# Another order table for a three-layer attention and MLP kernel on one core

## The chip, the cores and the metric

The kernel runs on one core of one Trainium2 chip. The time is the device time of one execution in microseconds. The kernel before takes 849.13 us (median of 3 runs, 848.77 to 849.22).

Six things work side by side in a core. TensorE (PE) multiplies matrices; its weight loads are listed as PEld. VectorE (DVE), ScalarE (ACT) and GpSimd (POOL) work element by element. SyncE (SP) issues the transfers of this kernel, and 16 DMA engines carry them out. Each engine works through its own list of instructions in order; an instruction that needs another engine's result waits at the head of its list, and everything behind it waits too.

## The reference, cut to what matters

```python
# q, k, v: (4, 8, 576, 64) float32
scores = (1/8) * q @ k.T
# heads 0-3: the last 32 positions; heads 4-7: every 4th of the last 128
scores = where(mask, scores, -1e9)
attn = softmax(scores)                        # over keys, + 1e-9 in the denominator
x = attn @ v                                  # -> (2304, 512)
h = x @ w_in;  g = relu(h)**2;      y1  = g @ w_out     # 512 -> 2048 -> 512
h = y1 @ w_in2; g = h*sigmoid(h);   out = g @ w_out2    # 512 -> 2048 -> 512
```

The four weight matrices come as 64-bit floats.

## The kernel before, in words

**Attention.** The 4 x 576 positions are eight halves of 288; each half has four pairs of heads, so there are 32 blocks. Of a block the kernel loads q, k and v (`load_blk`), multiplies q and k on TensorE (L533, "scores"), adds the mask and takes the row's extreme on VectorE (L558), exponentiates on ScalarE (L566, or L729 after a transpose for the first eight blocks), scales (L573, L575, L586, L590, L592, L754), transposes on TensorE (L602, L713, L715, L717) and multiplies by v (L625, L738). The first blocks subtract the extreme before the transpose (`less`, L691 on VectorE, L694 on GpSimd). Attention's matmuls are in fp32.

**Weights.** A piece of 128 x 512 weights arrives as 64-bit numbers (`raw`) and is turned into two fp32r parts, a high and a low one, whose sum it is (`weights`): the exponent and mantissa words are converted (L282 and L290 on ScalarE, L284 and L292 on VectorE or GpSimd), shifted (L302, or L304 on GpSimd), given their sign (L311, L314), added (L318), copied as the high part (L245 on ScalarE, L247 on VectorE, L249 on GpSimd: the helper `copy`) and subtracted for the low part (L252: the helper `sub`).

**First MLP.** Tiles of 256 tokens, three of them side by side (`mlp`): 12 fp32r matmuls of 256 columns per step S1 (L788 to L790: high x high, high x low, low x high), relu and square, split into high and low (L245, L252), and 12 per step S2 (L836 to L838). Attention and the conversion of weights run beside it. Then three tiles of 512 tokens (`mlp2`, L936, L990 to L992), in which products of sums of blocks save matmuls; the second MLP's weights are prepared at that time.

**Second MLP.** Three tiles of 768 tokens (`strassen`), with seven block products for eight, in steps of six matmuls of 384 columns (L1094 first, L1179 second product). Its halves are copied (L245, ScalarE) and subtracted (L252, VectorE or GpSimd; tiles `hl` and `gq`); prepared weights stream in as `ws`, `wa`, `wc` and `sw`.

**Order.** All this is 3,960 numbered operations. Nothing is planned when the kernel is built: a table, `ORDER`, lists them. `V1318` says that operation 1318 is issued to VectorE at this place of the program; A is ScalarE, G GpSimd, P TensorE, D a transfer on SP's queue. Numbers behind `@` are places of the buffers that the operation opens: a PSUM bank, or a place in a ring of SBUF. `F14@0` is a group of 14 warm-up matmuls on zeros (`filler`, L1245). A GpSimd operation also waits for the last VectorE operation before it in the table that is marked with `lock`. Waits between engines, and for a buffer's old readers, are derived from the tiles. So the table alone sets each engine's list, and which engine an operation goes to where several can do it.

Of the kernel before, what the change touches and what calls it, by code (L numbers as in the profile page):

```python
# [1358 lines left out]
V1 A3958 G0 F14@0 D3@140 D2@132 D33@136 V4 D64@144 D126@24 P5@20@0 F15@2 V8 V7 D34@148 V6 V18 D135@32 V9 V19  # L1359
P10@3 P36@28@1 V17 V50 P67@36@2 G20 A12 V38 A11 V49 V37 D65@156 V48 P13@0 V39 V68 V40 D95@152 P21@1 F3@3 V51 A22  # L1360
P41@2 A23 D96@160 V35 V14 P24@3 V71 A43 V15 G127@0 V70 A42 A16@2 V81 D398@196 V79 P52@1 V69 V82 P44@2 V80 A53
V25 A54 V72 A136@4 P55@0 V26 V45 V66 V46 A27 V83 D143@52 P98@40@3 V56 V138 A47@6 V57 P28@1 G129 P73@3 V100
A29@44 F3@2 V58 A74 V101 D160@76 P59@2 V111 A31@48 V99 P84@3 V32 A62 V30 A60 P75@0 A85 V102 V61 A128 F3@1 V63
V110 D152@56 P86@2 V76 V103 A137 V77 V112 P104@1 A78@8 V113 V87 F7@3 V97 V114 V88 A105 V130 D177@88 A89 P115@1
V139 P106@0 A116 V131 F1@2 P90@3 D169@80 P117@2 V140 A91@60 A93@64 A132@68 F5@1 V94 V92 A141@164 V107 V118
P400@3@1@72@0 V108 V119 D211@124 G133 A153@14 V109@12 V120 A162 V403 F2@2 V401 A145 P121@0 G142 V402 V410
D506@201 P404@2 V411 A122 A144@10 V123 V412 A154 V146 P1238@3 D186@92 V399 A161@2 V147 A170@0 V148 P413@1 A124
A405 V178@4 D220@128 A149@84 V125 V163 A1239@16 P406@0 V150 A414 A1240 V164 P415@2 A179 D194@108 V407 V155
P1244@3 A1241@6 V408 V165 A409@8 V416 V156 A166@100 D424@196 P507@0@1@96@1 V417 V1242 A418 V157 P1243 A1245@18
V167 A158@168 D151 V172 A1246 V510 A187@10 D134 P419@3 V159 P1250@2 A422@104 A420 V512 A1247@12 G189 V508 V423  # L1370
A513 V421 A171 D203@116 V1248 P426@3@0@112@2 V180 A1251@16 V173 A511 P1249 A509 V427 G174 V523 A1252 V428 A188
V429 V436 V438 A1253@14 P430@2 V525 A524 V437 V514 V521 A526 V515 V425 V1254 A522 P439@1 V190 A431 A516 V527
A517 V175@172 P432@3 V528 V176 A440 A529 P518@0 V530 A222 P441@2 V433 V181 A204@2 P531@1 P1255 V434 V442 A520
V182 A435@8 V443 V519 A533 V444 D539@196 A532 A183@120 V191 P534@3 A195@6 V184 P445@0 A537@12 A535 V446 P1256@1
A192@176 G197 V448 V536 A196 V447 D450@201 V449 V198 A205 V193 A1257@18 P540@0@3@20@3 A1258 V199 A1259@4 D237@40
A212@0 V1260 V554 A200@28 P1261 V556 G206 V545 A557 V558 V543 A555 D254@76 V541 V201 A559 P452@0@3@24@0 A542
V560 V207 A544 A546 V561 D538 V451 P1262@1 V208 D271@112 A562 A563 V547 V465 V548 V455 A549 V466 G550 V454
P564@2 V463 A1263@16 D228@36 V464 A565 V456 A1264 V453 A566 V209@180 P551@1 A1265@8 V214 P457@2 A552 A553 V210
A221@14 D245@72 P567@1 V215 A458 A213 V223 P467@0 V1266 A238@12 V216 P459@3 A568 A468 V224 D572@196 A570@4
A217@32 P469@2 V240 A229@10 V225 P1267 A256 V460 V470 V461 V471 G218 V462@6 A239 D478@201 V472 A246@8 V569  # L1380
P473@0 V231 P1274@1 A476@52 A474 V241 A230 V475 A226@184 D262@92 V477 V232 P573@3@0@56@1 A1275@18 V227 A1276
A1277@2 V233 D296@116 A255@6 P480@1@2@80@2 V589 V587 A234@88 G1278 V580 V593 V576 A590 V574 G235 V591 P1279 A247
V483 D305@24 V484 V482 A592 V481 V493 A575 V492 V494 A581 P485@0 V578 V491 A577 D202 V248 A588 V263@10 P495@3
A579 V242 A486 A594 V582 P1286@0 A243@188 V583 D279@108 V479 V595 V584 A272@0 V596 V249 P585@1 V597 A1287@16
P487@2 D219 V244 A586 A496 P598@1 V250 A1288 D571 P497@3 D288@124 A599 V488 A1289@2 V489 P600@0 A490@14 V498
# [288 lines left out]
```

## Time and profile before

| | |
|---|---|
| median of 3 runs | 849.13 us |
| profiled execution | 849.5 us |
| its span, first to last instruction | 847.7 us |
| busy: PE, DVE, ACT, POOL | 839.2, 638.8, 501.5, 122.2 us |
| DMA | 223.56 MB, 264 GB/s on average |

A span is the time between the first and the last instruction. Busy time is a union: instructions of one engine overlap at their ends. An engine's idle time matters only where another waits for it.

### The profile page before, as it was taken

The numbers are of one execution on the slowest core, as the hardware profiler recorded it, in microseconds if no ns is written. First come the engines' busy times: TensorE is split into PE (matmuls) and PEld (weight loads), VectorE is DVE, ScalarE is ACT, GpSimd is POOL, SyncE is SP. The second block draws the span as 40 slices with busy tenths as digits, with TensorE's granted clock in tenths as the row PEclk, the third lists the DMA queues.
The fourth block names the chain that finished last, engine by engine and source line by source line (L and its number), as shares of the span: only waits on it lengthen the run. The fifth ranks groups of instructions, "written<-read, shape, count | busy, mean of one in ns | idle before, by whom it ended". The sixth has DMA issues, their size and how long they took to land.

```text
span 847.7 us, 16967 instructions
## 1 busy us (share of the span) xinstructions
PE 839.2 (99%) x6009; PEld 795.6 (94%) x6009; DVE 638.8 (75%) x1706; ACT 501.5 (59%) x1324; POOL 122.2 (14%) x142
## 2 busy tenths in 40 slices
PE   9989999999999999999999999999999999999998
PEld 7879999999989889889998999999999999999998
DVE  6999999888888698768899997578722488422765
ACT  5999988887666265334542566565445555345652
POOL 2220000101210202131201002102201111202020
PEclk9999999999999999999999999999999999999999
DMA  9585568879898888988999989889774774773441
GB/s 344 178 284 207 152 204 304 278 265 333 310 303 318 308 292 282 326 311 288 336 344 299 343 308 351 301 287 324 248 259 149 246 266 164 269 262 111 174 159 65
DMA packets 83603, 223.56 MB, mean 264 GB/s; under 512 B 8768, under 2 KB 18240, under 8 KB 83520
## 3 DMA queue, kind: packets, MB, share of 16 engines
q1 hardware_dynamic: 83520, 222.49, 75.2%
q8 instruction: 47, 0.77, 0.3%
q14 instruction: 36, 0.29, 0.1%
HBM read 172.13 MB, written 50.33 MB: 262 GB/s over the span
## 4 chain that ended last, share of the span: by engine, by line
PE 94%; ACT 3%; DVE 1%; issue 0%; POOL 0%; POOLq 0%; ACTq 0%
PE y L1094 17%; PE sa L1179 15%; PE s L936 15%; PE y L1179 6%; PE y L990 5%; PE y L991 5%; PE y L992 5%; PE sa L1094 4%; PE s L788 3%; PE s L789 2%; PE s L790 2%; PE ax L533 2%; PE y L836 2%; PE ax L625 2%; PE y L837 2%; PE y L838 2%
## 5 line engine op out<-in xcount | busy, mean ns | idle before, releaser
L245 ACT CAST hl<-gq 128x384 fp32r<-128x384 f32 x168 | 79.5, 513 | 58.7 <-PE sa L1179 28.6
L1094 PE MATMUL y<-xs,ws 128*128 128x384 f32 x552 | 107.5, 334 | 0.0
L252 DVE TENSOR_TENSOR hl<-gq,hl 128x384 fp32r<-128x384 f32 x144 | 78.9, 581 | 27.3 <-ACT hl L245 24.0
L1094 PEld LDWEIGHTS y<-xs,ws 128*128 128x128 f32 x552 | 96.6, 188 | 0.1
L1065 DVE TENSOR_TENSOR gq<-y,gq 128x384 f32<-128x384 f32 x46 | 25.0, 554 | 94.1 <-PE y L1094 82.9
L1070 ACT COPY gq<-y 128x384 f32<-128x384 f32 x92 | 42.7, 479 | 75.0 <-PE y L1094 67.6
L1179 PE MATMUL sa<-hl,wp 128*128 128x384 f32 x432 | 79.1, 334 | 0.0
L936 PE MATMUL s<-x,ws 128*128 128x256 f32 x576 | 76.2, 284 | 0.0
L990 PE MATMUL y<-g,w 128*128 128x512 f32 x192 | 76.2, 397 | 0.0
L1179 PEld LDWEIGHTS sa<-hl,wp 128*128 128x128 f32 x432 | 75.2, 188 | 0.0
L991 PE MATMUL y<-g,w 128*128 128x512 f32 x192 | 75.2, 392 | 0.0
L992 PE MATMUL y<-g,w 128*128 128x512 f32 x192 | 74.9, 390 | 0.0
L952 DVE TENSOR_TENSOR h<-s,h 128x512 f32<-128x512 f32 x96 | 59.4, 619 | 19.8 <-PE s L936 16.6
L936 PEld LDWEIGHTS s<-x,ws 128*128 128x128 f32 x576 | 72.2, 191 | 1.2
L245 ACT CAST g<-r 128x256 fp32r<-128x256 f32 (+1 forms) x86 | 42.9, 504 | 51.2 <-DVE r L972 42.8
L566 ACT ACTIVATE ap<-ap,ast 96x128 f32<-96x128 f32 (+3 forms) x168 | 62.2, 371 | 8.3 <-DVE ast L575 4.2
L788 PE MATMUL s<-x,w 128*128 128x256 f32 x192 | 56.4, 294 | 0.1
L790 PE MATMUL s<-x,w 128*128 128x256 f32 x192 | 54.3, 283 | 0.0
L789 PE MATMUL s<-x,w 128*128 128x256 f32 x192 | 54.2, 282 | 0.0
L1179 PE MATMUL y<-hl,sw 128*128 128x384 f32 x288 | 51.4, 334 | 0.0
L1179 PE MATMUL sa<-hl,sw 128*128 128x384 f32 x288 | 50.9, 334 | 0.0
L1179 PEld LDWEIGHTS y<-hl,sw 128*128 128x128 f32 x288 | 50.0, 188 | 0.0
(176 smaller groups left out, 2071.2 us busy)
## 6 DMA issues: line engine op xcount, KB each, us to landing
raw<-w SPq DMA_DIRECT2D x64, 512.0 KB, 6.3
ws<-w1x SPq DMA_DIRECT2D x48, 512.0 KB, 6.7
ws<-w2x SPq DMA_DIRECT2D x48, 512.0 KB, 5.4
sw<-w2y SPq DMA_DIRECT2D x48, 512.0 KB, 4.5
wa<-w1s SPq DMA_DIRECT2D x24, 512.0 KB, 6.8
wa<-w2s SPq DMA_DIRECT2D x24, 512.0 KB, 5.7
w1x<-st SPq DMA_DIRECT2D x16, 512.0 KB, 4.8
w2x<-st SPq DMA_DIRECT2D x16, 512.0 KB, 5.1
```

The source lines that it names most:

```text
L245: self.nc.scalar.copy(out=out, in_=in_)
L252: self.eng[eng].tensor_tensor(out=out, in0=a, in1=b, op=ALU.subtract)
L566: es.append(self.op({"ACT": c_act(nk) + 0.185}, lambda e, i=i, n=n, c=c, p=p, st=st: nc.scalar.activation(out=p.tile[:n, c], in_=p.tile[:n ...
L788: nc.tensor.matmul(o, wh.tile[:, s], xh, start=(kk == 0), stop=False)
L789: nc.tensor.matmul(o, wh.tile[:, s], xl, start=False, stop=False)
L790: nc.tensor.matmul(o, wl.tile[:, s], xh, start=False, stop=(kk == KC - 1))
L936: nc.tensor.matmul(bank.tile[:, o:o + 256], wp, xp, start=i == 0, stop=last, skip_group_check=True)
L990: nc.tensor.matmul(o, wh.tile[:, s], gh.tile, start=c == 0, stop=False)
L991: nc.tensor.matmul(o, wh.tile[:, s], gl.tile, start=False, stop=False)
L992: nc.tensor.matmul(o, wl.tile[:, s], gh.tile, start=False, stop=(c == NF - 1))
L1094: nc.tensor.matmul(o, w[part == 2].tile[:, kk * P:kk * P + P], x[b][part == 1].tile[:, kk * half:kk * half + half], start=new and not kk a ...
L1179: nc.tensor.matmul(o, u.tile[:, c * P:c * P + P], v.tile, start=new and not q and not part, stop=q == nf - 1 and part == 2, skip_group_che ...
```

## The change

The table `ORDER` is replaced by another one; nothing else in the file differs. Each of the 3,960 operations is still there once. The 516 transfers stand in the same order as before. 180 operations are on another engine: 73 from ScalarE to VectorE, 55 from VectorE to ScalarE, 43 from GpSimd to VectorE, 9 from GpSimd to ScalarE. Of the 750 operations of TensorE 316 stand at another place in its list. The groups of warm-up matmuls have 45 matmuls in all, before 53. Most places of buffers are others. The start and the end of the table, before and after:

```diff
 ORDER = """
-V1 A3958 G0 F14@0 D3@140 D2@132 D33@136 V4 D64@144 D126@24 P5@20@0 F15@2 V8 V7 D34@148 V6 V18 D135@32 V9 V19
-P10@3 P36@28@1 V17 V50 P67@36@2 G20 A12 V38 A11 V49 V37 D65@156 V48 P13@0 V39 V68 V40 D95@152 P21@1 F3@3 V51 A22
...
+V1 F11@2 D3@111 D2@195 P5@13@0 G0 V6 V7 V8 V9 V17 V18 V19 D33@68 P36@88@1 V39 V37 D64@133 F11@1 V20 P21@1 A3958
...
-A3946@202 A3956 D3947 D3957
+V3932 P3929 P3933 P3937 D3911 D3913 D3847 P3941 P3945 P3948 P3949 A3946@83 D3947 P3950 P3951 P3952 P3953 P3954
+P3955 A3956 D3957
 """
```

In these lines 5, 36 and 67 are the scores of the first three blocks, 10 and 21 transposes of the first block, 12 and 22 exponentials, 20 the subtraction of the extreme of the first block's second head.

## Rows read from the trace of the kernel before

**Rows 1.** The page's first part: busy us, share of the span, instructions of each engine.
```profile
PE 839.2 (99%) x6009; PEld 795.6 (94%) x6009; DVE 638.8 (75%) x1706; ACT 501.5 (59%) x1324; POOL 122.2 (14%) x142
```
**Rows 2.** Stretches: length, busy PE, PEld, DVE, ACT, POOL, clock, DMA share, GB/s.
```profile
7.00:20.00 13.00, 12.41 (x155) 10.63 (x154) 10.96 (x81) 8.90 (x36) 3.33 (x5) 1.00 1.03 403
20.00:80.00 60.00, 56.64 (x579) 51.92 (x576) 58.37 (x248) 57.30 (x180) 10.52 (x12) 1.00 0.71 244
80.00:220.00 140.00, 139.88 (x1298) 134.12 (x1298) 128.41 (x414) 117.71 (x381) 6.08 (x10) 1.00 0.73 249
220.00:380.00 160.00, 160.00 (x1236) 142.28 (x1235) 126.75 (x383) 77.49 (x260) 33.38 (x41) 1.00 0.88 309
380.00:500.00 120.00, 120.00 (x734) 108.62 (x733) 110.39 (x192) 53.97 (x99) 14.12 (x18) 1.00 0.91 316
500.00:840.00 340.00, 340.00 (x1963) 339.91 (x1962) 202.42 (x382) 183.72 (x366) 53.11 (x47) 1.00 0.67 232
```
**Rows 3.** Waits of PE: line, waited for; us in total, times, longest.
```profile
PE y L837 <- POOL g L252: 0.9, 1, 0.9
PE y L836 <- ACT g L245: 0.8, 1, 0.8
```
**Rows 4.** Chain of waits in the last stage: start, us, what.
```profile
627.85 6.24 PE y L1094 x36
```
**Rows 5.** Timeline of the first 14 us, vector engines: start, us, what [idle before].
```profile
5.72 0.29 DVE L558 CUSTOM_DVE_ANT_0 ap<-y,mask 96x128 f32<-96x128 f32 x1 [2.39 <-PE y L533]
...
5.93 0.28 DVE L558 CUSTOM_DVE_ANT_0 ap<-y,mask 96x128 f32<-96x128 f32 x1
...
7.61 2.00 POOL L694 TENSOR_SCALAR ap<-ap,ast 96x96 f32<-96x96 f32 x3 [5.15 <-DVE ast L558]
...
9.11 0.29 DVE L558 CUSTOM_DVE_ANT_0 ap<-y,mask 96x128 f32<-96x128 f32 x1 [1.60 <-PE y L533]
...
10.58 0.47 ACT L729 ACTIVATE ap<-ax 96x96 f32<-96x96 f32 x2 [1.80 <-PE ax L713]
```
**Rows 6.** Timeline of the first 14 us, PE: warm-up matmuls, scores, transposes.
```profile
0.98 3.17 PE L1245 MATMUL fill<-warm 128*128 128x256 bf16 x14 [0.98 <-DVE warm L1237]
...
4.09 1.49 PE L533 MATMUL y<-w 64*96 64x96 f32 x12
5.51 2.52 PE L1245 MATMUL fill<-warm 128*128 128x256 bf16 x15
7.87 0.41 PE L713 MATMUL ax<-ident,ap 96*128 96x96 f32 x3
```
**Rows 7.** Timeline of PE where it turns between attention and MLP.
```profile
97.19 0.39 PE L788 MATMUL s<-x,w 128*128 128x256 f32 x1
97.41 0.28 PE L789 MATMUL s<-x,w 128*128 128x256 f32 x1
97.53 0.28 PE L790 MATMUL s<-x,w 128*128 128x256 f32 x1
...
245.16 0.87 PE L936 MATMUL s<-x,wc 128*128 128x256 f32 x6
245.96 0.72 PE L625 MATMUL ax<-ap,blk 96*64 96x96 f32 x12
```
**Rows 8.** Groups by line and form: busy us, mean ns of one, idle before.
```profile
L284 DVE TENSOR_SCALAR cv<-raw 128x512 f32<-128x512 f32 x18 | 7.5, 419 | 2.6 <-DMA raw<-w 2.3 <-PE zx L838 0.3
L290 ACT ACTIVATE raw<-raw 128x512 int32<-128x512 uint32 x50 | 33.2, 679 | 2.9 <-DMA raw<-w 2.9
L252 DVE TENSOR_TENSOR hl<-gq,hl 128x384 fp32r<-128x384 f32 x144 | 78.9, 581 | 27.3 <-ACT hl L245 24.0 <-POOL hl L252 2.7
L252 POOL TENSOR_TENSOR hl<-gq,hl 128x384 fp32r<-128x384 f32 x24 | 25.7, 1076 | 155.2 <-DVE hl L252 53.5 <-ACT hl L245 45.2 <-DMA wa<-w2s 33.6
```
**Rows 9.** Transfers into tile sw: us from issue to landing.
```profile
DMA to landing us min/median/max: 3.5/4.5/9.9
```

More of the change, by code (lines that the diff above doesn't have):

```diff
@@ L1364 @@
[L1364 to L1373, printed above, removed]
@@ new lines @@
+A1299@153 A1300 A297@148 V603@156 V257 V265 V258 V503 V290 V505 P1268@3 A1269@146 A1270 A1271@5 D605@73
+P606@2@1@14@3 V602 V274 V275 D638@9 A298 A264 P1280@0 A1281@93 V259 V620 V622 V624 V626 V1272 V607 A608 A260@192
+A1282 A1283@41 G1284 V282 V609 V283 V613 V261 V266 P1292@3 D322@56 D604 A1293@22 A289@108 D313@80 P639@1@36@2
+V641 V645 V611 V273 P640@0 V654 V291 A1301@201 A1294 A324 A614 A1295@146 A306@0 A610 V1551@7 V267 V643 A612 A646
+P1273 P1285 A642 A644 P1304@1 A621 V1302 V284 V1296 A268@128 A307 A655 V285@40 V652 V656 V615 V269 A623
@@ new lines @@
+A1305@150 A625 P1303 A657 A627 A653 P1310@2 V616 V617 P618@3 V286 V299 V647 V1550@162 V276 V658 V659 P1322@0
+V628 V629 P1297 D339@124 D185 A619 A1306 A1311@94 A1307@138 A1312 V648 A649 A660 V1554@156 V630 P631@2 A632
+V1308 P1309 V1552@110 V308 A277@132 V292 D666@201 V1553 V293 V278 V294@136 D287 A1323@153 P661@3 A1313@5 A1324
+A1325@151 V1326 P633@1 P650@2 V300 V1314 V295 V301 A651 A636@21 A662 A634 A315 P1316@0 A1317@116 D637
+P667@3@76@1 V671 P668@2 A1318 A1319@20 P663@0 V684 A1556 A664@93 V669 V635 V673 V682 A685 V680 V1320 V1555 P1315
@@ new lines @@
+A865 P1459 D2079 D2080@76 D909@196 P1430@2 A1431@90 V1639 V1641 V1632 P877@3 A878 P879@3 V1650 V1651 A1432
+A1463@110 A1433@85 V1659 V1434 A1652@20 A880@60 D881 D1633 V397 V1653 D1654 P1466@2 A1676 A1467@113 V1468
+A1469@108 V1470 P1472@3 A1473@15 V1474 A1475@17 P1435 A1528@100 V1526@89 A1530@61 V1660 V1464 D1527 D1529
+V1661@20 V1662 V1666@82 D1531 D2081 P1484@3 A1485@49 A1486 P1478@2 A1479@46 A1532@80 A1487@9 A1643 P1490@3
+A1491@74 A1492 V1664@128 V1488 P1471 P1465 V2088@61 V1665 V1667 V1476 V1644 D882@201 D2125@40 D1533 D1663 A1480
@@ new lines @@
+P910@2@3@44@0 V913 V915 P1507 A1536@13 A2095@60 V922 V911 V1512 D1541 A2086@84 V924 V926 D1682 V2083 D1539 D1537
+A923 A912 A914 A916 V917 V918 V919 P906@2 A907@68 A925 D908 V2096 A927 V928 D1670 D936@201 P1514@3 P920@2 A921
+V929 V930 V2099 P1513 A1515@121 A1516 P931@2 A932 A1517@18 P1520@3 A1521@52 A1522 A1523@4 D2127@0 P933@2
+A934@105 V1684@30 V1685 P2154@3 D967@196 D935 D1702@21 V2085 P2155@2 V1686 V1687 V2087 V1688 V1692@116 V1693
+A1689@34 V1694@6 A2158@11 V1518 V1695 P2156@3 V2159 V1524 P2157@2 P1519 V1690 V2160 V2161 V2162 V2170@97
@@ new lines @@
+D1698 D1545 V1044 A2201@64 V1715 V1035 A1034 V2204@128 P2186 P2190 P1061@3@2@23@2 A1049 V2202 P2203 V1716
+V1722@28 A1045 A1036 V1031 A1032 V1046 A1047 V1079 V1037 V1050 V1077 V1051 A1053 V1081 A1082 V1068 V1038 V1062
+A1063 V1066 V1052 A2205@95 A1067 V1064 V1040 V1075 D1549 D1730@104 D2138@8 A1731@12 A1078 P2208@2 P1054@0 A1055
+V1039 P1041@3 D1028 P2209@1 V1720@108 V1721 V1056 V1723 A1043 A1065 V1042 P1057@0 V2206 P2207 P2210@3 A1069
+A1080 A1732 G1733 V1070 V1071 V1072 G1717@39 V1718 D2135@20 D2141@116 D2148@64 D1091@196 A1076 V1083 V1084
@@ new lines @@
+A2212@49 V2213 V1058@15 A1727 V1734 P1073@2 V1085 P1086@0 P2211@1 A1087 A1074 V1735 V1728 V2214 V2215 V2216
+V2217@0 P1092@2@0@68@2 V1106 V1108 P1088@3 A1089@43 V1099 V1093 V1097 V1095 V1110 V1112 A1724 V1725 D2146@80
+D2139@130 D1739@4 P2225@1 P2226@3 A1094 A2229@95 A2218@45 A1741 D2143@92 D1719 V2219 V1740@36 V1742 P2227@0
+P2228@1 P2242@2 P2220 D2144@19 D1729 D2150@56 V2230 A1100 A1096 A1098 V1101 V1102 V1103 V2231 V2232 P2243@0
+P1104@3 A1113 A1107 V2233 D1059 D1726 D2149@104 D2100@116 D2145@128 D1090 D1122@201 D2328@76 V2221@0 A2222@52
@@ new lines @@
+P2254 D2153@56 P2278@2 V1137 A2280@68 A2111@128 V1135 V2119@124 V2281 A2269@108 A2256@80 V1139 V2257 A1138
+A2104@104 A1140 D2327@15 D1738 D2332@48 A2120@88 D1754 D1767@112 D2329@52 D2330@36 V2105 V2113@11 V2274 V2282
+V2283 P2279@1 V2284 P1150@3@0@60@3 A2114@116 A1125 A1129 V1162 A1127 A1163 P2258 A2106@64 V1759@22 V2289@19
+V2270 P2271 P2275 V1164 A2290@2 A1136 A1165 V1130 V1131 V1151 V2285@73 V2107 D2341@84 V1166 V1761 A1132 P1133@2
+D1757 D2333@24 V2291 V1141 A2108@80 V2109 V2115 A2286@32 V2116@102 P2358@0 V1142 V1153 V2287 V1155 A1156
@@ new lines @@
+V1925 V2639 V1926 D1895 D2547@120 D1956@80 A1848@12 V1927 V2640 V1849 D1921 D2554@108 D2552@32 D2553@28
+D2508@172 D2557@126 D1948@122 V1935 V2627 V1938@72 V1939 A1942 A1950 A1949@0 V1957@18 V1940@184 P2636@0 P2650@3
+P2651@2 D1918 D1850 V2641 V2642@169 V1941 V1928@178 D2509 A2654@92 A2643@24 A1945 G1929 D2551@61 V1958 V1959
+D2510@96 A1902@197 V2646@119 G2647@57 V1946 V2655 V1951 V1952 P2628 P2652@3 P2653@0 P2667@1 P2632 A2671@193
+D1982@88 D2556@65 V1943 V2648 D1947 A2512@180 D2511 D2560@40 D2561@11 D1944 D2558@188 V1903 V1953 V2656 V2644
@@ new lines @@
+V2529 V1988@142 D2749@67 P2794 P2796 V2797 P2799@3 A2793@16 P2801 P2803 V2800 A2795@19 P2806 A2802 V2018@92
+V1855 V1995 V1856 A1997 A2020 V1998 D2026@148 V2014@156 G2019 A2028 A2023 A2027@100 D2707 D2709 D2739@2 D2705
+V1860@88 V2791 D2034@160 G1862@46 V1861 V1863 A1867 D2746@96 V2024 P2808 A2809@28 P2810 P2812 V2813 V2021
+V2006@154 D1999 D2743@140 D1996 A2036 A2811@43 P2815@1 P2817 P2819 A2820 P2822 A2798 A2818 A2804 A2821 V2029
+V2807 V2030 V1868 V2007 V1857@80 V1858 D2753@63 V2816 V1989 V2031 V2032@148 A2035@0 V2037 P2824 A1864 P2826
@@ new lines @@
+P2902 A2975@94 A2894 P2904 P2921 P2924 V2970 V2903 A2072 V2073 V2905 P2907 D2770@119 A2901 A2906 A2928@91
+A2945@136 V2929 V2956 P2927 P2930 P2934 P2938 D2712@66 D2767@123 D2074 D2714@81 D2768@127 D2771@115 D2769@174
+D3155@6 D2713 A2908 A2909 A2939@105 V2946 A2957@151 V2948 A2949@11 A2953@87 V2940 P2941 V2950 A2942@190 V2954
+V2978 A2979@180 A2075 A2943 A2971@78 P2947 V2982 V2958 V2990 V2960 P2951 P2955 P2959 A3004@97 V2976 V2980
+A2961@75 V2986 V2964 A3007@131 V3008 V2962 D2772@0 A2987@183 A2965@89 V2966 P2963 P2967 A2968@175 V2994
@@ new lines @@
+A3068@100 V3038 V3069 V3096 V3042 D3175@12 D2781@118 D3171@8 D2715 D3154@104 D3163@14 A3057@122 A3045@87
+A3086@125 V3046 A3074@58 A2719@112 V3030 V3054 P3039 P3043 V3050 P3047 P3051 P3055 V3058 P3059 A3071@92 V3075
+V3060 A3083@3 V3084 V3028 A3089@186 A3061@131 V3062 V3116 A3117@97 P3063 P3070@0@3 V3118 V3078 V3072 P3073 V3090
+V3108 A3080@0 V3081 V3087 V3100 V3120 V2720 D3031 D3167@173 D3183@180 A3097@151 V3098 P3076 P3079 V3104
+A3105@161 P3082 D3158@136 D3029 D3160@93 P3085 P3088 V3124 D3156@37 V3066 V3064 V2728 V3106 A3101@131 V3102
@@ new lines @@
+A3381@22 D3557@180 D3188@189 P3354 V3366 V3316 A3329 V3374 V3382 A3359@186 V3360 V3396 V3410 V3390 V3406 A3433@2
+V3398 V3404 A3424@131 A3326 V3384 D3192@88 D3552@64 G3434 D3189@56 P3358 P3361 P3367 P3371 P3375 P3379 P3383
+V3414 A3385@74 V3464 A3391@5 D3191@96 D3134@28 A3442@122 A3362@190 A3363 A3407@173 V3392 V3386 V3418 V3408
+A3419@125 A3415@22 V3416 A3427@128 A3399@186 V3400 V3425 A3411@112 A3430@10 V3431 V3412 D3561@14 D3569@8
+D3193@115 D3565@0 P3387 P3393 P3397 P3401 P3405 V3443 V3476 V3420 P3409 P3413 P3417 P3421 D3194@103 A3436@74
@@ new lines @@
+A3668 V3663 P3669 A3670 P3672 P3674 P3676 P3678 A3677@161 P3681@1 A3675@151 D3576@122 D3575@187 D3578@116
+D3577@176 V3679 V3650 P3683 P3685 P3688 A3686 D3579@130 D3582@104 D3583@112 A3684 V3634 V3673 A3655 A3734@101
+A3664 V3666 V3682 A3648 V3689 P3690 A3691@68 P3692 A3693@71 P3694 V3695 A3687 D3580@172 P3697@3 P3699 P3701
+A3702 P3704 P3706 P3730@1@2 A3671 A3737@122 A3740@190 A3703 A3743@7 A3750@116 A3700 V3735 A3707@22 A3754@187
+V3755 V3762 A3680 P3708 V3705 A3709@25 A3763@126 P3733 P3710 V3711 P3713@0 V3738 V3766 V3741 P3715 A3716 V3764
```

416 lines of the change are left out of this document (181 added, 235 removed).

## The prediction

> **What bounds the kernel now.** I read the page's head first: TensorE is busy for 839.2 us, 99% of the span of 847.7 [rows 1]. Then the stretches [rows 2]. From 220 to 840 us TensorE has no idle time at all, while VectorE has 33 us free in 220 to 380, 9.6 in 380 to 500 and 138 in 500 to 840. The chain of waits in the last stage is TensorE alone, 36 matmuls of 384 columns in 6.24 us, 0.173 us each [rows 4]; nothing that the change touches alters the number of these matmuls, so 92% of the time can't be won, only lost. What is left is the front. Between 20 and 80 us VectorE is busy 58.37 of 60 us and ScalarE 57.30, TensorE only 56.64: there the two vector engines feed it, and it stands for 0.9 us on a GpSimd subtraction and 0.8 us on a ScalarE copy at most [rows 2, 3]. Between 80 and 220 us TensorE is full again (139.88 of 140) but VectorE has only 11.6 us free, so the cover is thin.
>
> The profiled execution took 849.5 us, 1.8 more than its span; the median of the runs shown is 849.13. I make the sum as a difference and take it off the median.
>
> **The change part by part.** Only the table of the order is new. Beside it the same 3,960 operations run; the 516 transfers keep their order on SP's queue. I count what moves between engines by where the operation started in the trace of before, and price it by rows: a conversion on VectorE lasts 0.419 us, on ScalarE 0.679 [rows 8]; two VectorE instructions that follow each other start 0.21 apart though the first lasts 0.286, so one occupies the engine for some 0.075 less than its row says [rows 5], 0.34 us here; on ScalarE I take off 0.1 likewise and get 0.58.
>
> *First 80 us.* Ten operations go from ScalarE to VectorE (six conversions, two normalisations of three and four units, two small copies), five come back (four of 512 columns, one small), one GpSimd subtraction (the entry 20) goes to VectorE and one conversion to ScalarE. VectorE: 6 x 0.34 + 0.7 + 0.5 for the small copies + 0.5 for entry 20 - 4 x 0.34 - 0.14 = +2.2 us. ScalarE comes out at -2.6, GpSimd at -2.7. VectorE is the fuller engine and has 1.6 us free from 20 to 80, so 2.2 more don't fit there; but there are 2.0 more free from 7 to 20 [rows 2]. Of these, 1.60 is one wait at 9.11 us, for the scores of the third block (entry 67), which stand on TensorE behind the second block's scores, the transposes of entry 10 and 15 warm-up matmuls that last to 7.87 [rows 5, 6]. In the new table the second scores follow straight on the first, 11 warm-up matmuls come behind them, and VectorE has the second block's reductions to do while it waits; this wait should go. What is late next is entry 10: its transposes wait for the second group of fills, so ScalarE starts at about 8.8 instead of 8.3, but then without the 1.80 us wait at 10.58 [rows 5]. If none of the 3.7 us free behind the start is recovered, the front gets 2.2 longer; if all is, 1.5 shorter. I take 2.5 recovered (the wait and half of the rest): -0.3. The GpSimd subtraction itself (2.00 us for three [rows 5]) goes into 0.5 of VectorE, and is in that sum.
>
> *Fills.* 53 become 45. Later matmuls of as many columns take 0.12 us [rows 7], 8 of them 1.0. They stand where TensorE would wait anyway, so nothing to -1.0; I take nothing, since in the front it is the vector engines that are late.
>
> *80 to 220 us.* 24 operations go from ScalarE to VectorE and 19 back, one leaves GpSimd: VectorE +1.7, ScalarE -4.0, on a VectorE with 11.6 free. Between 0 and +1.7; I take 0, because the free time is six times as long. If that cover is gone, the matmuls of the first MLP wait for the subtraction that makes their low half.
>
> *220 to 500 us.* 220 to 380: VectorE +4.0 of 33 free, ScalarE +2.1, GpSimd -16.3. 380 to 500: VectorE +5.9 of 9.6 free: eleven conversions and seven copies from ScalarE, six from GpSimd, five back. It would be at 97%. From 0 to +5.9; I take 0, because much of what was added prepares weights for the stage after 500, and can slide there.
>
> *500 to 840 us.* 20 subtractions of 384 columns leave GpSimd (1.076 us each) for VectorE (0.581 [rows 8], 0.5 occupied), with some others VectorE +11.6 us of 138 free. TensorE has no gap to close: 0. The buffers behind sw are placed anew: between the last reader of one and the first use of its next content there were at least eight steps of six matmuls (8 x 1.04 = 8.3 us [rows 4]), now at five places seven (7.3). Such a transfer lands in 4.5 us, in the worst burst in 9.9 [rows 9]. So 0, with 2.6 (9.9 - 7.3) as the other end, once.
>
> *Order on TensorE.* 316 of its 750 operations stand at another place, most by one to four. What that changes is how often it turns from fp32 attention work to the MLP's matmuls. The first matmul after attention's holds the array for 0.22 us, the next for 0.12: 0.10 lost at a return. Before scores or products six matmuls take 0.80 us where 0.72 would do: 0.08 [rows 7]. In the table before there are 85 returns and 39 turns into scores or products, now 81 and 37: 4 x 0.10 + 2 x 0.08 = -0.5 us. Most of them lie where TensorE is full, so this counts whole (0 to -0.6).
>
> Sum: -0.3 + 0 + 0 + 0 + 0 - 0.5 = -0.8 us; 849.13 - 0.8 = **848.3 us**.
>
> [...] The first 14 fills, of 256 columns each, take 3.11 us up to the first scores, 0.22 each [rows 6]; later ones of that width take 0.12 [rows 7]. That is 1.2 and then 2.4 GHz, and the second group, 15 in the 2.36 us to 7.87, holds the rise (0.16 each), after TensorE had worked almost without a gap from 0.98. In the new table 11 fills instead of 14 come first, so there will be some 0.6 us of nothing before the block lands. [...]
>
> **The rivals.**
> *Later clock.* If TensorE stays at 1.2 GHz over the second group of fills and the next small operations, 11 x 0.10 for the fills and 0.4 each for two sets of transposes, twice the 0.41 of a set [rows 6], make ScalarE's start 2.0 us later, of which its wait of 1.80 hides a part that I can't tell: up to -0.8 + 2.0 = +1.2, 850.3. For it: the gap. Against it: the scores of two blocks now follow each other, which is denser work. 0.05.
>
> *The front gets shorter.* All 3.7 us of free VectorE time are recovered (-1.5), the fills count (-1.0) and the turns (-0.5): -3.0, 846.1. For it: the attention blocks are fetched earlier relative to their use in the new table (counted along TensorE's list, the narrowest cases had 4.4 to 6 us of work between the buffer's release and the scores, four of these six now 12 or more), and ScalarE, 95% busy from 20 to 80, loses 2.6 us. Against it: VectorE has more to do, not less; before the first MLP matmul it now has 84 operations to get through instead of 76. 0.30.
>
> *VectorE's queue sets the pace (slower).* The waits of before are replaced by others, so that its 2.2 in the front and the 1.7 from 80 to 220 us come out whole: 3.9 - 0.5 = +3.4, 852.5. It decides when VectorE is busy for over 98% from 20 to about 150 us and TensorE's idle time there stands behind VectorE instead of GpSimd and ScalarE. For it: 97% is reached already. Against it: the 11.6 us free. 0.16.
>
> *A late transfer (slower).* One sw or ws load lands behind its use, 2.6 - 0.8 = +1.8, 850.9, or more if several do. Against it: medians far under 7.3. 0.06.
>
> That the change doesn't do what it says isn't a case: the table is the program.
>
> **How the numbers follow.** Forecast 0.43, later clock 0.05, shorter front 0.30, VectorE's queue 0.16, late transfer 0.06. 0.2% is 1.7 us, about what a measurement can tell from no change. Faster by more than that: the shorter front, 0.30. Within: the forecast and the later clock, 0.48. Slower: the last two, 0.22. The forecast's own range is 847.4 to 850.0 (VectorE's recovered time between 1.6 and 3.4 and a little of the thin covers). The range for 8 in 10 takes in the shorter front with 0.9 more and nearly all of VectorE's case: 845.3 to 852.2.
>
> **What would show it.** Right: TensorE without idle time from 80 to 840 us, VectorE's wait near 9 us gone, VectorE busy 2 us more in the first 80, total VectorE some 25 us and GpSimd some 53 us off (up and down), the first MLP matmul about 1 us later than before though the front ends no later. Wrong: idle time of TensorE behind VectorE or a transfer after 80 us; a clock that rises after 7 us with ScalarE's start beyond 10; or a front that ends 2 us earlier.

## The result and the profile after

The changed kernel takes 854.72 us (median of 4 runs, 854.33 to 857.35), the kernel before 849.08 in the same comparison: a ratio of 1.0074 [1.0053, 1.0094], 5.6 us slower. Forecast were 848.3 and 845.3 to 852.2. The profiled execution took 857.35 us, the slowest of the four, with a span of 855.4, 7.7 us longer than before's.

The page's first part for the changed kernel [rows 1], then the stretches, columns as in [rows 2]:

```profile
PE 843.5 (99%) x6002; PEld 798.4 (93%) x6002; DVE 660.8 (77%) x1768; ACT 493.8 (58%) x1300; POOL 74.9 (9%) x82
```

```profile
7.00:20.00 13.00, 12.80 (x133) 10.19 (x131) 10.88 (x84) 7.83 (x31) 1.52 (x2) 1.00 1.02 402
20.00:80.00 60.00, 56.30 (x560) 51.84 (x560) 55.44 (x230) 53.30 (x162) 12.35 (x11) 0.94 0.70 239
80.00:220.00 140.00, 138.70 (x1287) 132.96 (x1283) 131.18 (x433) 116.91 (x379) 7.70 (x9) 1.00 0.70 242
220.00:380.00 160.00, 159.90 (x1255) 142.95 (x1254) 135.48 (x397) 80.35 (x269) 16.66 (x17) 1.00 0.88 305
380.00:500.00 120.00, 120.00 (x735) 108.04 (x734) 107.81 (x195) 44.27 (x82) 10.85 (x11) 1.00 0.89 318
500.00:840.00 340.00, 339.84 (x1954) 338.28 (x1953) 214.87 (x417) 186.93 (x374) 24.17 (x22) 1.00 0.68 237
```

The totals moved about as forecast (VectorE +22.0, GpSimd -47.3). What is new is the 0.94 of the clock in 20 to 80 us, and 1.3 us of idle TensorE in 80 to 220, where before had 0.12. What TensorE waits for, in the whole execution [rows 3]:

```profile
PE ax L602 <- POOL ap L592: 1.6, 1, 1.6
PE y L533 <- DMA w<-qkv: 1.5, 2, 0.8
PE fill L1245 <- DVE warm L1237: 1.0, 1, 1.0
PE ax L713 <- DVE ap L691: 0.8, 1, 0.8
PE s L788 <- ACT xo L245: 0.7, 2, 0.5
PE ax L625 <- ACT ap L245: 0.5, 1, 0.5
```

The two waits of before are gone. The longest is now for a GpSimd normalisation (L592, entry 550: two units of 96x128). Its place in the timeline: start, us, engine and instruction, in brackets the idle time ahead of it. The second POOL line is the second unit alone:

```profile
53.48 0.68 DVE L311 SCALAR_TENSOR_TENSOR cv<-raw,cv 128x512 int32<-128x512 int32 x1
54.08 0.42 DVE L302 TENSOR_SCALAR cv<-cv 128x512 int32<-128x512 int32 x1
54.42 0.68 DVE L252 TENSOR_TENSOR w<-cv,w 128x512 fp32r<-128x512 f32 x1
55.03 0.41 DVE L302 TENSOR_SCALAR cv<-cv 128x512 int32<-128x512 int32 x1
...
57.26 0.69 DVE L318 CUSTOM_DVE_ANT_0 cv<-raw,cv 128x1024 uint16<-128x1024 uint16 x1 [1.81 <-ACT raw L290]
...
53.01 2.67 POOL L592 TENSOR_SCALAR ap<-ap,ast 96x128 f32<-96x128 f32 x2 [4.18 <-ACT ap L590]
53.36 2.32 POOL L592 TENSOR_SCALAR ap<-ap,ast 96x128 f32<-96x128 f32 x1
...
55.74 0.39 PE L602 MATMUL ax<-ident,ap 96*128 96x96 f32 x1 [1.57 <-POOL ap L592]
```

The same two units took 0.72 us in the kernel before, beside VectorE's reductions (L558):

```profile
50.69 0.26 DVE L558 CUSTOM_DVE_ANT_0 ap<-ax,mask 72x104 f32<-72x104 f32 x1
...
50.62 0.72 POOL L592 TENSOR_SCALAR ap<-ap,ast 96x128 f32<-96x128 f32 x2 [3.07 <-ACT ap L590]
```

Here four conversions follow each other on VectorE from 53.48 to 55.44, and GpSimd's second unit ends at 55.68, 0.24 after the last. TensorE stands for 1.57 us, and then its granted clock is 0.50 for 6.8 us, in which matmuls of 256 columns start 0.21 us apart instead of 0.12 (the profile gives the clock as a share of full speed alone; the gigahertz of the recorded texts are rough estimates from 256 columns in 0.22 and in 0.12 us). Length, busy of PE, PEld, DVE, ACT, POOL, granted clock, DMA:

```profile
50.00:55.80 5.80, 3.97 (x44) 3.45 (x41) 5.45 (x29) 4.46 (x20) 2.67 (x2) 1.00 0.93 345
55.80:62.60 6.80, 6.80 (x48) 6.45 (x49) 3.86 (x12) 5.24 (x13) 1.29 (x1) 0.50 0.38 112
62.60:80.00 17.40, 17.25 (x199) 16.32 (x197) 16.40 (x71) 15.14 (x48) 2.04 (x2) 1.00 0.90 301
```

The start, TensorE and then ScalarE's first exponential [rows 5, 6]:

```profile
0.98 2.53 PE L1245 MATMUL fill<-warm 128*128 128x256 bf16 x11 [0.98 <-DVE warm L1237]
4.29 1.49 PE L533 MATMUL y<-w 64*96 64x96 f32 x12 [0.78 <-DMA w<-qkv]
6.49 1.49 PE L533 MATMUL y<-w 64*96 64x96 f32 x12 [0.71 <-DMA w<-qkv]
7.92 2.53 PE L1245 MATMUL fill<-warm 128*128 128x256 bf16 x11
10.55 1.10 PE L713 MATMUL ax<-ident,ap 96*128 96x96 f32 x6
...
11.30 0.86 ACT L729 ACTIVATE ap<-ax 96x96 f32<-96x96 f32 x4 [9.08 <-PE ax L713]
```

Both scores wait for their block's transfer, all 22 fills shown take 0.23 us each, the clock rises at 11.43 us instead of 7.00, and ScalarE starts 3 us later. At these two times the trace's record of the clock begins, at 1.00, and the column above counts what lies ahead of it as 1.00 too; six transposes take 1.10 us from 10.55 us on and 0.72 from 12.26 on. (The new table has 46 warm-up matmuls in all, not the 45 given with the change: TensorE runs 6,002 instructions against 6,009.)

To see where TensorE loses time without a long wait, I matched every step of TensorE to its entry in the table and took, step by step, the time to the next step's start beyond what the fastest eighth of such steps took in the kernel before; fills count whole. I call it TensorE's loss, in us by stretch (profiled executions):

| kernel | 0-20 | 20-60 | 60-110 | 110-220 | 220-500 | 500- | sum | span |
|---|---|---|---|---|---|---|---|---|
| before | 10.2 | 7.8 | 4.4 | 5.1 | 6.1 | 0.05 | 33.7 | 847.7 |
| after | 11.8 | 10.2 | 4.2 | 6.6 | 6.7 | 1.3 | 40.8 | 855.4 |
| v550 | 10.7 | 7.6 | 3.1 | 7.0 | 6.2 | 1.5 | 35.9 | 850.1 |
| lean_v | 10.5 | 7.3 | 3.1 | 6.6 | 6.2 | 1.3 | 35.0 | 849.1 |
| swaps | 10.9 | 7.6 | 3.6 | 8.9 | 6.3 | 1.4 | 38.7 | 852.8 |
| swaps_lean | 10.9 | 7.6 | 3.0 | 8.3 | 6.1 | 1.3 | 37.2 | 851.4 |
| late_stage | 10.7 | 7.3 | 3.2 | 7.0 | 6.2 | 1.0 | 35.3 | 849.5 |

Losses and spans differ between kernels by the same amounts within 0.6 us, so the table accounts for the time. Three stretches lost: 0 to 60 us, 110 to 220, and the last stage.

### The profile page after: what moved, and what is told of

The parts are those of the page before. It is cut to its first block, busy times and chain, and to the rows that moved or that the text cites. A ratio compares the mean times of both kernels' runs of the same rounds, so it can differ in the third digit from the quotient of the medians.

```text
span 855.4 us, 16881 instructions
## 1 busy us (share of the span) xinstructions
PE 843.5 (99%) x6002; PEld 798.4 (93%) x6002; DVE 660.8 (77%) x1768; ACT 493.8 (58%) x1300; POOL 74.9 (9%) x82
## 5 line engine op out<-in xcount | busy, mean ns | idle before, releaser
L252 DVE TENSOR_TENSOR hl<-gq,hl 128x384 fp32r<-128x384 f32 x160 | 85.3, 570 | 38.7 <-ACT hl L245 38.3
L245 ACT CAST hl<-gq 128x384 fp32r<-128x384 f32 x168 | 77.3, 512 | 51.8 <-DVE gq L252 19.5
L952 DVE TENSOR_TENSOR h<-s,h 128x512 f32<-128x512 f32 x96 | 59.5, 620 | 10.9 <-PE s L936 5.7
L245 ACT CAST g<-r 128x256 fp32r<-128x256 f32 (+1 forms) x91 | 45.4, 507 | 34.5 <-DVE r L972 26.6
L252 DVE TENSOR_TENSOR g<-r,g 128x256 fp32r<-128x256 f32 (+1 forms) x87 | 47.5, 550 | 5.1 <-ACT g L245 4.4
L1179 PE MATMUL sa<-hl,sw 128*128 128x384 f32 x288 | 50.9, 334 | 0.0
```

What stands on the lines that cost most here:

```text
L245: self.nc.scalar.copy(out=out, in_=in_)
L252: self.eng[eng].tensor_tensor(out=out, in0=a, in1=b, op=ALU.subtract)
L952: add = lambda o, a, b: nc.vector.tensor_tensor(out=o, in0=a, in1=b, op=ALU.add)
L1179: nc.tensor.matmul(o, u.tile[:, c * P:c * P + P], v.tile, start=new and not q and not part, stop=q == nf - 1 and part == 2, skip_group_che ...
```

## The experiments

Kernels that ran together share the chip and the runs of before (medians 848.7 to 849.4 from one such group to the next); kernels of different groups compare to about 0.7 us. All are edits of the table's words.

**Order or engines?** Two kernels: the new order with the old engines, and the old order with the new engines.

```diff
-A209 (order of after)      +V209 and the 179 others as before   (order_only)
-V209 (order of before)     +A209 and the 179 others as after    (engines_only)
```

> The new table's order and buffer places, but each operation on the engine that it had before. Theory A (the loss of 5.6 us is in the order: the start, where the second block's scores stand ahead of the fill matmuls and the clock rises at 11.4 instead of 7.0 us, some 2 us; the place of one GpSimd normalisation, entry 550, beside VectorE's conversions at 53 us, 1.6 us; small stalls later): 852 to 855 us, high clock from about 11.4 us. Rival B (the loss is VectorE's added work, +2.2 us up to 80 and +1.7 from 80 to 220): 849.0 to 850.5. Half of it left, 851 to 852, means both.

> The table's order and places of before, but each operation on the engine that it has in the new table. Theory A: no later clock and 849 to 850.5 us. Rival B (VectorE's added work and the operations taken from GpSimd cost by themselves): 852 to 855 us, with TensorE waiting behind VectorE between 20 and 220 us.

order_only: 891.84 us, 1.0493 [1.0474, 1.0513]. engines_only: 859.06, 1.0114 [1.0097, 1.0130]. Neither expectation holds: each half alone is worse than both together. So the price of a moved operation depends on the order around it, which my prices by row left out. In order_only TensorE's waits are of every kind:

```profile
PE ax L602 <- ACT ap L590: 2.9, 3, 1.7
PE s L788 <- ACT xo L245: 2.6, 4, 1.3
PE y L1094 <- ACT gq L1070: 2.6, 1, 2.6
PE ax L625 <- DVE ap L247: 2.0, 2, 1.4
```

**The start.**

```diff
-F11@2 .. P5@13@0 .. D33@68 P36@88@1 V39 V37 D64@133 F11@1 V20 P21@1 .. P10@2
+F14@2 .. P5@13@0 .. D33@68 D64@133 F15@1 P10@2 A3958 A12 A11 P36@88@1 V20 P21@1 ..
```

> The changed kernel, with TensorE's first group as before: 14 fills, the first scores, 15 fills, the transposes of entry 10, then the second block's scores (26 of VectorE's and ScalarE's words follow in the order that this needs). Theory A: the high clock comes at 7 to 8 us again, ScalarE's first copies at 8.3 instead of 11.3, and the time falls by 1.5 to 2.5 us to 852.2 to 853.2. Rival B (the front is bound by VectorE's work up to 80 us, a late start is caught up): the clock comes earlier too, but the time stays at 854.2 to 855.

854.70 us, 1.0098 [1.0062, 1.0133] (854.03 to 862.29; three of its seven runs took 862 us, with a mean granted clock of 0.986): the clock is high from 5.3 us (the first 14 fills take 0.22 us each, the 15 from 5.44 us on 0.11), ScalarE's first exponential comes at 7.53, 3.8 us earlier, and the time stays. The same on a base without the wait at 54 us (`both`, below) gives 853.42 against 852.96. The first part of theory A is refuted. GpSimd reaches entry 550 at 51.3 us here and at 50.9 in fed (below), which has the new start: by then the head start is gone. What takes it back isn't shown.

**Entry 550.**

```diff
-A549 G550 P551@3
+A549 V550 P551@3
```

> The changed kernel with one word changed: entry 550, a normalisation of two 96x128 units, on VectorE instead of GpSimd. Theory A: TensorE's wait of 1.57 us at 54.2 us goes, and with it the fall of the clock from 55.8 to 62.6 us that the profiled run showed: 1.4 to 1.8 us less than the changed kernel's undisturbed runs, 852.9 to 853.3, and no run at 857. Rival B: VectorE, the fuller engine, takes on 0.34 us, so 854.5 to 855.

852.96 us, 1.0043 [1.0026, 1.0060], 1.8 less than after by the medians; the wait and the fall of the clock are gone. Confirmed. In its timeline the six transposes of the two entries, 564 and 551, run without a gap:

```profile
52.44 0.74 PE L602 MATMUL ax<-ident,ap 96*96 96x96 f32 x6
```

It is the order that holds GpSimd up: the two units take 2.67 us in order_only too, and 0.72 in engines_only. Whether VectorE's neighbours cause it is the next run:

```diff
-V215 V223 V210 V451 V240 D572@92 A213 V216 V224
+V215 V451 D572@92 A213 V216 V223 V210 V240 V224
```

> The changed kernel with three of VectorE's words (entries 223, 210, 240: two shifts and a subtraction of 512 columns) behind entry 216, so that VectorE has nothing to run from 54.2 us while GpSimd works on entry 550. Nothing moves to another engine. If GpSimd's normalisation is held by VectorE's instructions that run one behind the other: it takes about 1.5 us instead of 2.67 (until the last of them, entry 215, ends), TensorE's wait falls from 1.57 to 0.3 to 0.5 us, and the time by 1.0 to 1.3 us, to 853.4 to 853.8. If GpSimd is slow by itself there (its two instructions, or its queue): 2.67 us again and no gain, 854.5 to 855.

Timeline of GpSimd, then of TensorE:

```profile
52.63 1.39 POOL L592 TENSOR_SCALAR ap<-ap,ast 96x128 f32<-96x128 f32 x2 [4.19 <-ACT ap L590]
...
54.08 0.30 PE L602 MATMUL ax<-ident,ap 96*128 96x96 f32 x1 [0.29 <-POOL ap L592]
```

1.39 us, until 54.02, 0.23 after entry 215 ends, and a wait of 0.29: both are as expected. The time isn't: 854.78, 1.0072 [1.0057, 1.0087]. VectorE's list is late a little further on, and TensorE stands there instead:

```profile
PE y L837 <- DVE g L252: 1.1, 1, 1.1
```

And the clock:

```diff
-G550 P551@3
+G550 F12@3 P551@3
```

> The changed kernel with one word added: a group of 12 fill matmuls of 256 columns on TensorE right ahead of entry 551, the transposes that wait for GpSimd's entry 550. At 2.4 GHz they take 12 x 0.12 = 1.4 us of the 1.57 to 1.84 us that TensorE stands there. Theory F (the clock falls because TensorE stands at 54 us): the wait stays as long with the fills in it, but the clock stays at 2.4 GHz after 55 us in all runs (it fell in 9 of the 15 runs that had this wait and in none of the 28 without it), no run above 855.5, median 854.2 to 854.8. If the fall comes from what follows (the small transposes and matmuls up to 61 us): it falls again in most runs.

```profile
51.46 0.41 PE L602 MATMUL ax<-ident,ap 96*96 96x96 f32 x3
51.71 1.47 PE L1245 MATMUL fill<-warm 128*128 128x256 bf16 x12
53.33 0.58 PE L602 MATMUL ax<-ident,ap 96*96 96x96 f32 x3
...
50.88 2.67 POOL L592 TENSOR_SCALAR ap<-ap,ast 96x128 f32<-96x128 f32 x2 [4.17 <-ACT ap L590]
```

853.68 us, 1.0048 [1.0033, 1.0063]. GpSimd takes 2.67 us again and TensorE still can't go on before 53.3, but with fills in the gap the mean granted clock is 1.0 in all five runs, and the time is half a microsecond better than expected. Counting runs with 0.998 or less: 6 of 8 of after and spread, which have the bare wait, and 1 of 65 of the kernels with the new start and no such wait. (start_back and both show lower clocks at a second place: both's profile has a granted clock of 0.50 from 13.5 to 30.5 us; the expectation's count included these.) So here the fall comes from TensorE standing there (1.57 us in after). From the start of 564, the transposes ahead of the wait, to the end of 473 the steps take 10.1 us in after, 7.7 in fed, 6.2 in v550: the half clock is worth 2.4 us in the profiled execution, the wait 1.5.

**110 to 220 us.** At three places the new table has taken out the step that stood on TensorE between a step and the one that needs it: 723, 728, *1357*, 1382; 817, *833*, 1442; 877, *1430*, 879. 1382 and 1442 open the PSUM bank that ScalarE's copy of 723 and 817 has still to empty, 879 needs the copy of 877. TensorE loses 0.49, 0.57 and 0.70 us there; in before the steps at these places lose 0.18 or less, only 833 0.35; together 1.8 us against 0.7.

```diff
-P1382@2 A1383@126 A1384 P1357          +P1357 P1382@2 A1383@126 A1384
-P1442@3 A1443@93 V831 V832 P833@2      +P833@2 P1442@3 A1443@93 V831 V832
-P1430@2 .. V1632 P877@3                +P877@3 P1430@2 .. V1632
```

> The changed kernel with three pairs of steps on TensorE put back as they stood before: entry 1357 ahead of 1382, 833 ahead of 1442, 877 ahead of 1430. Theory C (the new order puts a step of TensorE right behind the one whose result it needs through a ScalarE copy: 723 and 1382 share a bank, so do 817 and 1442, and 879 needs 877's transposes copied; TensorE stands 0.49, 0.57 and 0.70 us there): the three waits go, 1.5 to 1.8 us less than the changed kernel, 852.9 to 853.3. Rival B (VectorE or ScalarE is the pace of 80 to 220 us, so that the waits come out one step later): 854.2 to 854.8, with TensorE's idle time of 110 to 220 us unchanged in sum.

> The changed kernel with entry 550 on VectorE and the three pairs on TensorE as before. If the two losses are in different stretches and TensorE has no cover in either, they add: 854.7 - 1.7 - 1.7 = 851.3 us (851.0 to 851.7). If the later one only takes up what the first leaves: 852.5 to 853.

> As the one before, and in the last stage two copies of ScalarE (entry 2809 and what follows it) ahead of three conversions (2023, 2027, 1867) that wait for a GpSimd addition (2019), as TensorE's entry 2817 stands 0.34 us for 2809's copy at 512 us, and some 0.6 us in all within 505 to 530 us: 0.4 to 0.6 less than the one before, 850.7 to 851.0 us. If the small gaps of the last stage have another cause: no less, 851.3.

In these three runs 833 runs ahead of 831 and 832, the normalisations that it needs, so it transposes values that aren't scaled yet. spread: 855.68, 1.0082 [1.0056, 1.0108]; fix2: 853.17, 1.0055 [1.0040, 1.0070]; fix3: 853.87, 1.0059 [1.0044, 1.0074]. No gain, as rival B has it: other waits come one step later (0.63 at 1382, 0.75 ahead of 877, 0.99 ahead of 879 in spread). But two of these the edit itself makes: 740, which now follows 1382, opens the bank of 1382, and ScalarE's copy 878, for which 879 waits, stayed behind ScalarE's 1431, which needs 1430. So these runs don't decide between C and B; swaps, below, has neither fault. fix3's second edit cut the loss after 500 us from 1.29 to 0.87, too little for the times to show. Is it the load of an engine?

```diff
 (on v550)
-V302 V311 V314 V328 V345 V366 V370    +A302 A311 A314 A328 A345 A366 A370   (relief)
-A332 A341 A348 A357 A358              +V332 V341 V348 V357 V358             (load)
 start_back's edit, on v550                                          (both)
```

> The changed kernel with entry 550 on VectorE (853.0 us measured, the base of this run) and seven weight conversions of 98 to 140 us (302, 311, 314, 328, 345, 366, 370) back on ScalarE, where they were before: VectorE 7 x 0.34 = 2.4 us less, ScalarE 4 us more. Theory D (with 68.3 of 70 us busy from 80 to 150, VectorE is the pace there; it has 1.7 us free where before had 3.75): TensorE's waits of 110 to 190 us (2.4 us beyond its best in 110 to 190 where before had 0.2 behind idle time) fall by 0.8 to 1.8 us, 851.3 to 852.2. Rival E (the chain attention makes through ScalarE's copies and exponentials is late): no less or more, 853 to 854.5.

> The same base, the suspected cost made larger: five conversions of 110 to 130 us (332, 341, 348, 357, 358) from ScalarE to VectorE, 5 x 0.34 = 1.7 us more on VectorE, 3 us less on ScalarE. Theory D: VectorE's 1.7 us free are used up, TensorE waits 0.8 to 1.7 us longer, 853.8 to 854.7. Rival E: ScalarE's copies come earlier, 852.3 to 853.

> The same base, with TensorE's first group as before (14 fills, first scores, 15 fills, the transposes of entry 10, then the second block's scores). The high clock comes at 5 to 7 us instead of 9 to 11, ScalarE's first copies at 7.5 instead of 11.3. If the late start is paid for in full (theory A): 1.5 to 2.5 us less, 850.5 to 851.5. If the vector engines, busy to 97% from 20 to 80 us, take the gain back: 852.6 to 853.2.

relief: 855.45, 1.0069 [1.0053, 1.0086]; load: 854.59, 1.0055 [1.0035, 1.0076]. Worse both ways, so taking work off one engine for the other doesn't help, whichever it is. With relief ScalarE's copies come later, and the wait for the copy `xo` grows from 0.8 us in two pieces to 2.3 in three (below); with load a block of attention is fetched late, and TensorE stands 1.1 us for the transfer.

```profile
PE s L788 <- ACT xo L245: 2.3, 3, 1.3
```

both: 853.42, 1.0067 [1.0037, 1.0097], 851.75 to 862.29: the start is worth nothing that these runs can tell. Then work taken away without moving any:

```diff
 (on v550: words left out)
-V291 V299 V308 V316 V325 V333 V342 V350 V359 V367 V376 V384 V393   (lean_v)
 (on lean_v)
-A307 A315 A341 A332 A358 A375         +V307 V315 V341 V332 V358 V375 (lean_both)
```

> The changed kernel with entry 550 on VectorE (the base, 853.0), and 13 shifts of the weight conversion (entries 291 to 393, at 80 to 160 us) left out, so that the low bits of these weights are wrong in what it computes: VectorE has 13 x 0.34 = 4.4 us less in 80 to 160, nothing is moved. Theory D (VectorE is the pace of 80 to 190): TensorE's waits there, 2.4 us more than before had, fall to under 1, 851.0 to 852.2. Theory C (TensorE's order: three steps stand for 0.50, 0.57 and 0.70 us right behind the one whose result they need, whatever VectorE does): these three waits stay, 852.5 to 853.2.

> As the one before, and six conversions (307, 315, 341, 332, 358, 375) from ScalarE to VectorE: VectorE 13 x 0.34 - 6 x 0.34 = 2.4 us less than the base, ScalarE 6 x 0.58 = 3.5 us less. If the two engines together are the pace of 110 to 220 us (taking work from one and giving it to the other made it worse both ways): more of the waits go than with VectorE relieved alone, 850.8 to 851.8. Theory C: the three waits stay, 852.5 to 853.2.

TensorE's waits in 110 to 220 us, of v550 and then of lean_v (whose lines are numbered two higher):

```profile
PE s L788 <- ACT xo L245: 0.8, 2, 0.5
PE ax L625 <- ACT ap L245: 0.5, 1, 0.5
```

```profile
PE ax L627 <- ACT ap L247: 0.5, 1, 0.5
PE s L790 <- ACT xo L247: 0.5, 1, 0.5
```

lean_v: 852.32, 1.0035 [1.0024, 1.0045]; lean_both: 852.05, 1.0032 [1.0022, 1.0042]. Both lie between the ranges that were given, and neither is clear of v550. With 4.4 us less on VectorE the loss at 817 and 877 is 0.57 and 0.70 as in v550; only the first of the three waits, at 728, goes. This fits theory C at two places and theory D at the third. The last two runs ask whether the old places would do with the new load, with 833's normalisations moved along:

```diff
 (on v550; swaps_lean also without lean_v's 13 words)
-P740@2                                    +P740@3
-P1442@3 A1443@93 V831 V832 P833@2         +V831 V832 .. P833@2 P1442@3 A1443@93
 (and the two other pairs as in spread, A878 right behind P877)
```

> The changed kernel with entry 550 on VectorE (853.0), and the three pairs of TensorE's steps as before: 1357 ahead of 1382 (and 740 on the other bank, as before), 833 ahead of 1442 with its two normalisations 831 and 832 ahead of VectorE's conversions, 877 ahead of 1430. Theory C alone (only TensorE's order matters): the waits of 0.50, 0.57 and 0.70 us go, TensorE's loss in 110 to 220 us falls from 6.95 to 5.2 (before had 5.12), 851.2 to 851.7. Theory C with D (the order makes the waits, but the new place of each step also fits how late VectorE and ScalarE are there): other waits come in their place, loss 6.5 to 8, 852.5 to 853.5.

> The same three pairs, and the 13 shifts of the weight conversion left out as in the earlier run (4.4 us less on VectorE in 80 to 160; the low bits of these weights are wrong in what it computes; that run had 852.3 and a loss of 6.57 in 110 to 220 us). Theory C alone: 5.0 to 5.3. Theory C with D: here the vector engines are early enough for the old places, so the waits do go, loss 5.0 to 5.5 and 850.8 to 851.3, though they did not without the relief. If waits come in their place here too: 6 or more; then it is ScalarE's place in the order that decides.

swaps: 855.66, 1.0070 [1.0049, 1.0092]; swaps_lean: 854.18, 1.0057 [1.0036, 1.0077]; losses in 110 to 220 of 8.9 and 8.3. The third outcome: even with VectorE early the old places make it worse. The third pair is mended (0.19 instead of 0.70), but 740, after 1382, now stands 0.94 us for VectorE in swaps (0.3 in swaps_lean), and 833 about a microsecond in both. Timeline of swaps ahead of 833:

```profile
165.26 0.62 ACT L245 CAST w<-cv 128x512 fp32r<-128x512 f32 x1
165.52 0.22 DVE L558 CUSTOM_DVE_ANT_0 ap<-ax,mask 72x72 f32<-72x72 f32 x1
165.67 0.08 DVE L558 DVE_READ_ACCUMULATOR2_ANT ast<- 72x1 f32 x1
...
165.87 0.21 PEld L602 LDWEIGHTS ax<-ident,ap 72*72 72x72 f32 x3 [1.14 <-ACT w L245]
165.90 0.29 PE L602 MATMUL ax<-ident,ap 72*72 72x72 f32 x2 [0.98 <-ACT w L245]
```

The profile puts this wait down to a weight copy of ScalarE, but TensorE's weight load starts at 165.87, before that copy ends at 165.88. What ended just before, at 165.75, is VectorE's reduction from the bank that 833 opens; in VectorE's list it stands behind 833's normalisations, which in turn need ScalarE's exponentials (VectorE stands 0.35 us for them in swaps_lean). Which engine's order would have to change for the old places to do is not shown.

**The last stage.**

```diff
 (before) the 20 subtractions hl and gq: -G +V                       (hl_moved)
 (on v550) -G2019 -G1862 +V2019 +V1862, P2808 A2809 ahead of A2023   (late_stage)
```

> The kernel before, with only the 20 subtractions of 384 columns of the last stage from GpSimd to VectorE, each at its place in the order. My sum has them at nothing (10 us onto 138 free): 849.1, within 0.5 of before, no idle time of TensorE from 500 to 840. If VectorE's queue there makes TensorE wait, as the small gaps of 1.3 us in the changed kernel's last stage might mean: 850 to 851.

> The same base, and in the last stage the two GpSimd additions 2019 and 1862 on VectorE, and ScalarE's copy 2809 ahead of the conversions 2023, 2027 and 1867 that wait for them (ScalarE stood 2.2 us for GpSimd at 508 us). If these hold the 1.3 us of TensorE's small gaps in 500 to 690 us: TensorE's loss there falls to 0.4 to 0.7 us, of which the order alone gave 0.4; 852.1 to 852.6 us. If the gaps come from the other operations of the last stage: 0.9 or more is left.

hl_moved: 848.94, 0.9995 [0.9986, 1.0004]. Moving the subtractions costs nothing, with TensorE full:

```profile
500.00:840.00 340.00, 340.00 (x1963) 339.91 (x1962) 207.79 (x400) 182.94 (x365) 32.46 (x27) 1.00 0.66 232
```

late_stage: 852.39, 1.0033 [1.0024, 1.0043]. ScalarE's wait in 500 to 530 us on v550,

```profile
ACT st L245 <- POOL st L417: 2.2, 1, 2.2
```

is gone, and the loss falls from 1.5 to 1.0, not to 0.4 to 0.7. A third of the gaps came from there; the rest has another cause, which I did not find. By its median it is the fastest version of the new table that leaves nothing out, though not clear of v550, and still 0.3% behind before.

## Why the prediction was wrong

**Order on TensorE: the step that failed.** The sum has one term for the order, and I put it at -0.5 us by counting the turns between attention and MLP; a wait that new neighbours make had no term, on TensorE or on the other engines. What counts is which steps stand next to each other. One pair of neighbours on two other engines (a GpSimd normalisation and VectorE's conversions) cost 1.8 us by the medians, and in the profiled execution another 2.4 by the clock; v550, pause550 and fed show this. Three pairs on TensorE stand for 1.8 us in 110 to 220 us, where the same steps lost 0.7 before; no run won this back, so its cause is open in part. In the last stage 1.3 to 1.5 us are lost. All these places could be read from the two tables beforehand; I counted them for transfers alone. The -0.5 for the turns is measured by no run.

**"92% of the time can't be won, only lost": a misreading.** The stretch from 220 to 840 us is 73% of the span, and there full time did get lost, in the last stage.

**First 80 us: -0.3.** Without entry 550 this is near: up to 110 us v550 has lost 21.4 us and before 22.4. I priced GpSimd by what leaves it, and overlooked what happens to what stays.

**The wait at 9.11 us goes: wrong**, it moved to 12.36 us (1.45 long), for the same reason as the later-clock rival gives. That rival came true in the profiled execution, at the place that I named: rise at 11.43 us, ScalarE at 11.30. That the shorter first group of fills put the rise off is not shown: lean_both has the same first instructions, and its clock rose at 4.7 us. The rival's price of 2.0 was too high: over 14 profiles with the new start the loss up to 20 us goes with the rise, from 9.8 (rise at 4.7 us) to 11.8 (11.4), 0.3 us for each us.

**80 to 220 us: 0.** v550 lost 1.9 us more than before from 110 to 220 us, and 0.7 less from 80 to 110: 1.2, within the 0 to 1.7 of this term, but not by its mechanism. VectorE was at 98% from 80 to 150 us in v550, about what the rival at 852.5 asked for there (from 20 to 80 us it was at 92% in after), and yet lean_v gave back only 0.4 of this loss.

**220 to 500 us: 0** held (0.1 in v550). **500 to 840: 0** held for what was priced (hl_moved), not for what wasn't: of the 1.3 to 1.5 us a third is one GpSimd addition, issued ahead of ScalarE's conversions, that holds up a copy for TensorE. **Transfers: 0** held; TensorE waits for none after the start of the changed kernel. **Fills: 0** can't be told apart: start_back has the old first groups and is no faster.

Left open: why the start pays so little, beyond that VectorE and ScalarE are busy to 92% and 89% from 20 to 80 us in after; 1.0 us in the last stage; and whether a version of the new table without the two waits at 817 and 877 would be faster: VectorE's and ScalarE's order there would have to be rewritten as well, and no run does that.

## What to carry to other kernels

When only an order changes, compare neighbours: for each step of the critical engine, the distance to the step whose result it needs through another engine's copy, and to the last use of its PSUM bank; here a step too few stood for 0.5 to 0.7 us. For each GpSimd instruction that stays, look at what VectorE will run beside it; here the same two units took 0.72 us or 2.67. Order and engine choice are one thing: a price for a moved operation holds only in a stage where nothing waits for it.

## What the runs showed of the hardware

**GpSimd stood while VectorE's conversions followed each other.** The two units of entry 550 took 0.72 us beside reductions from PSUM (before), 2.67 beside four conversions (after), 1.39 beside one (pause550), the last two ending 0.24 and 0.23 us after the last conversion. In after GpSimd didn't get in between the four: its second unit, recorded from 53.36 us, 0.12 ahead of the first conversion, lasted 2.32 us, through all of them. What in the conversions held it is not shown.

**Behind a wait of 1.57 us TensorE's granted clock was halved for longer than the wait.** It was 0.50 for 6.8 us in after and for 3.4 in start_back; spread, which has the wait too, had a mean of 0.997 in its profiled run. With fills in the gap the mean was 1.0 in all five runs of fed. With waits of 1.3 us in relief and 1.1 in load it was 1.0 in the profiled runs.

**With the same first instructions the clock rose between 4.7 and 11.4 us.** How long the scores waited for their transfers doesn't tell when: 1.4 us in all in lean_both, with the rise at 4.7, and 1.5 in after, with the rise at 11.4. The spread is 6.7 us.
